# A Fourier layer with a routed mixture of experts: small VectorE steps of gate, ranks and scales fused or given to GpSimd, the inverse's result evicted by either of two engines, constants anew

## The chip, the cores and the metric

The kernel runs on one core of a Trainium2 chip. The metric is device time in microseconds (us), the median of three runs. Five engines work side by side: TensorE (PE in the profile, its weight loads PEld), VectorE (DVE), ScalarE (ACT), GpSimd (POOL) and SyncE (SP), which issues most transfers.

## The reference, cut

```python
def _attn_ref(x, w_r, w_i, b_r, b_i):             # x: 8 x 2496 x 256
    X = np.fft.rfft(x, axis=1)
    Yr = X.real @ w_r - X.imag @ w_i + b_r
    Yi = X.real @ w_i + X.imag @ w_r + b_i
    Y = soft(Yr, 0.01) + 1j * soft(Yi, 0.01)      # sign(v) * max(|v| - 0.01, 0)
    return np.fft.irfft(Y, n=2496, axis=1)

def _moe_ref(x, w_gate, w_output_gate, w1, w2):   # x: 19968 x 256; 8 experts, 1024 wide
    logits = x @ w_gate
    e_idx = np.argmax(logits, axis=1)
    gate_w = softmax(logits)[range(N), e_idx]
    eom = 1 / (1 + exp(-(x @ w_output_gate)))
    for e in range(8):
        m = e_idx == e
        out[m] = gate_w[m] * eom[m, e] * (relu(x[m] @ w1[e]) @ w2[e])
    return out
```

## The kernel before

**Two parts.** Up to about 546 us the kernel runs the Fourier layer and the routing; after it the experts' matmuls. Numbers of full precision are carried as pairs of f16 (a high part and the rest), so most products are three matmuls, and most results are evicted from PSUM by two engines: ScalarE writes the high part, VectorE the rest.

**The Fourier layer** goes batch by batch (8 of them), several batches in flight. A batch's 2496 = 39 x 64 points are transformed in two steps: `stage1_pair` (matmuls L722, evicted into `at` by ScalarE L741 and VectorE L742), a turn (transposes L803 into `A`, evicted by L807 or L808, ScalarE or VectorE), `stage2` (matmuls L839, evicted into `xt` by L850 and L851). Then `mix`: ScalarE seeds a PSUM bank with the bias (L871), PE adds the spectral products onto it (24 matmuls of L895 to a bank), ScalarE and VectorE make the soft threshold (L914, L915), L921 to L923 split it, PE does the inverse's first step (L931, L937, L940; 12 short matmuls to a bank), and that is evicted into `bt` by ScalarE L955 and VectorE L956 and into the short `ste` by L957 or L958. PE cannot start L895 of a bank before its seed, and ScalarE does its instructions in the order of its queue. `stage4` does the inverse's second step (L1006); its result `yt` is evicted by ScalarE alone (L1010, 88 times in all) and stored.

**Gate, ranks, scales.** For each batch `scales` works out powers of two for its values, `gate` the softmax, the chosen expert as a one-hot tile (`goh`, and `oh` as f16) and the factor `gf`; `rank` counts each token's place within its expert: PE sums the one-hot tile over tokens (L1124 to L1129, using the pair sums `two` and `four`), VectorE adds what earlier batches counted (`cnt`) and splits the rank into a part above 128 (`rhi`) and a part below (`rlo`). Nearly all of these are VectorE instructions on tiles of 117 x 22 or 117 x 176. `weights` scales the experts' sixteen weight blocks: two ScalarE squares a block (L1189), the maximum over partitions by a diagonal (L506), one matmul and a reduce, and then a high and a low part of each quarter (L1207 to L1212, ScalarE, GpSimd or VectorE), stored to DRAM.

**The experts.** 160 tiles of 128 tokens are gathered (GpSimd's indirect DMA, L1575), split, turned by DMA, and multiplied by `w1` (L1712) and `w2` (L1671), in two phases: 64 tiles of the first four batches, then the rest, for which `routing` runs again meanwhile.

**What sets the order.** The order of every engine's instructions is worked out when the kernel is built, by a planner (class `Issue`): each step asks for an engine with a due time and an assumed duration, and an engine that is free takes, of what is ready, the step that is due first. The due times are sums of constants (`P`, `SD`, `YE` and so on). A step may offer several engines, each with a constant of its own, and the first that takes it does it.

Of the kernel before, what the change touches and what calls it, by code (L numbers as in the profile page):

```python
# [153 lines left out]
S2 = 36.19
E1 = 82.57
DS = 4.85
ES = 34.56
Z1 = 12.24
SD = 132.3
Z2 = -21.33  # L160
IV = 103.61
IS = 2.48
GO = -1340.85
R0 = 141.78
R1, G1 = -1014.28, 0.61
GA = 0.73
W0 = 43.28
W1 = 19.43
TG = 1016.93
# [15 lines left out]
LR = 1668.96  # L185
QN, QY, QV, QX, QZ, QU = 3866.14, 1364.73, 1212.64, 805.81, -550.14, 1685.64
RA, QE = 1801.63, 933.82
SA = 944.74
SE = 31.03
Z3 = 233.71  # L190
BE = 2815.69
YE = -619.08
PB = 0.39, 14.59, 85.72, 5.95, 22.66, 102.66, 62.64, -123.59
O0 = 1223.31, -1027.38, 1422.52, -7.66, 35.14, -414.49, 54.41, 251.39
O1 = 1875.42, -636.5, -63.9, -292.47, 1069.7, -70.5, 1004.15, 899.13
O2 = 1839.52, -6.84, 1018.92, -1092.03, 4.43, 1897.44, 1747.57, -106.55
O3 = -364.35, -986.35, -931.95, -936.43, -1557.73, -1082.43, -727.4, 454.49
O4 = -1854.58, -1035.4, 1670.63, 1274.07, 1014.79, -952.98, -211.38, -1425.86
# [3 lines left out]
WF = -1.9
QO = 909.37
WHL = 850.77
RG = 1206.15
QG = 1153.73
# [1576 lines left out]
```

## Time and profile before

| | us |
|---|---|
| median of 3 runs | 1391.66 |
| lowest, highest | 1390.07, 1393.12 |
| profiled execution | 1396.24 |
| its span, first to last instruction | 1394.5 |
| mean granted clock of TensorE | 0.997 |
| TensorE busy | 1368.5 (98%) |
| VectorE busy | 981.9 (70%) |
| ScalarE busy | 749.3 (54%) |
| GpSimd busy | 611.8 (44%) |

The profiled execution took 4.58 us more than the median, and 1.74 us more than its span. The busy shares are averages over the two parts of the kernel, which have different limits; the table of stretches tells them apart. In a timeline "idle before" is the time for which the engine stood still ahead of the instruction, with the instruction that ended it behind the arrow.

### The profile page before, as it was taken

How to read it: one execution, taken by the hardware profiler on the slowest of the kernel's cores; microseconds unless marked ns; L12 is line 12 of the kernel's file. 1: busy time of each engine (PE TensorE's matmuls, PEld its weight loads, DVE VectorE, ACT ScalarE, POOL GpSimd, SP SyncE). 2: the span in 40 equal slices, each digit the busy share in tenths (PEclk: the TensorE clock that was granted, in tenths of full speed). 3: DMA queues.
4: the chain of work that ended last, by engine and by line, in shares of the span. 5: the costliest groups of instructions: out<-in, count | busy, mean ns of one | idle time of the engine just before them, and what ended most of it. 6: DMA issues, size and time to landing. Idle time of an engine off the chain costs nothing.

```text
span 1394.5 us, 40372 instructions
## 1 busy us (share of the span) xinstructions
PE 1368.5 (98%) x15528; PEld 1229.4 (88%) x15528; DVE 981.9 (70%) x2852; ACT 749.3 (54%) x1443; POOL 611.8 (44%) x703
## 2 busy tenths in 40 slices
PE   8999999999999999999999999999999999999998
PEld 8998898898888888898998988899999899999997
DVE  6888888889998977788888865554555455554551
ACT  6778787978787764433333343433333343433342
POOL 2374446446676642354444434333333333333322
PEclk9999999999999999999999999999999999999999
DMA  8597999998997889884452464454542655537540
GB/s 248 133 219 215 205 243 213 255 226 207 256 211 179 192 257 170 254 203 138 130 137 74 114 157 117 102 167 108 166 105 73 170 156 140 138 74 200 129 118 30
DMA packets 280546, 231.11 MB, mean 166 GB/s; under 512 B 233076, under 2 KB 242039, under 8 KB 273954
## 3 DMA queue, kind: packets, MB, share of 16 engines
q1 hardware_dynamic: 264735, 186.68, 53.7%
q0 software_dynamic: 15344, 41.77, 11.6%
q8 instruction: 122, 2.00, 0.6%
q14 instruction: 71, 0.57, 0.2%
q10 hardware_dynamic: 274, 0.09, 0.0%
HBM read 285.30 MB, written 58.45 MB: 247 GB/s over the span
## 4 chain that ended last, share of the span: by engine, by line
PE 83%; DVE 5%; issue 5%; ACT 3%; DMA 2%; POOL 1%; SPq 0%; POOLq 0%; DVEq 0%; ACTq 0%
PE ps L1712 28%; PE ps L1671 28%; PE ps L895 12%; PE ps L722 4%; PE ps L1006 3%; PE ps L839 3%; PE ps L940 2%; PE ps L937 1%; POOL out L1691 1%; PE ps L1474 1%; PE ps L1052 1%; DMA x<-in_x 1%; ACT junk L1189 1%; DVE bt L956 1%; DVE xt L851 0%
## 5 line engine op out<-in xcount | busy, mean ns | idle before, releaser
L1671 PE MATMUL ps<-wbuf,hh 128*128 128x256 f16 x3408 | 415.2, 273 | 0.0
L1712 PE MATMUL ps<-eT,wbuf 128*128 128x256 f16 x3408 | 412.9, 273 | 1.2 <-issue 0.7
L1723 DVE SCALAR_TENSOR_TENSOR hh<-ps,hh 128x512 f16<-128x512 f32 x284 | 196.1, 690 | 262.6 <-ACT hh L1722 218.1
L1712 PEld LDWEIGHTS <-wbuf 128*128 128x128 f16 x3408 | 330.3, 98 | 44.2 <-issue 6.0
L1671 PEld LDWEIGHTS <-hh 128*128 128x128 f16 x3408 | 330.7, 98 | 38.8 <-issue 0.4
L1722 ACT ACTIVATE hh<-ps 128x512 f16<-128x512 f32 x284 | 169.6, 597 | 338.4 <-PE ps L1712 294.0
L1691 POOL DMA_INDIRECT out<-o,sidx x160 | 163.0, 1019 | 260.3 <-ACT o L1688 232.4
L1575 POOL DMA_INDIRECT yg<-yd,gidx x160 | 158.5, 991 | 262.0 <-DVE yhl L1602 219.6
L895 PE MATMUL ps<-whl,xt 128*128 128x256 f16 x1824 | 213.6, 274 | 4.4 <-ACT ps L871 4.2
L895 PEld LDWEIGHTS <-xt 128*128 128x128 f16 x1824 | 176.5, 98 | 27.8 <-issue 5.2
L1688 ACT ACTIVATE o<-ps,facs 128x256 f32<-128x256 f32 x160 | 75.9, 474 | 96.3 <-PE ps L1671 83.1
L1601 ACT ACTIVATE yhl<-yg,ys 128x256 f16<-128x256 f32 x160 | 78.6, 502 | 51.5 <-DVE ys L484 14.5
L722 PE MATMUL ps<-f1t,x 117*128 117x120 f32 (+1 forms) x704 | 85.0, 277 | 2.0 <-DVE at L742 1.8
L722 PEld LDWEIGHTS ps<-f1t,x 117*128 117x128 f32 x704 | 82.0, 192 | 4.8 <-DVE at L742 2.8
L1602 DVE SCALAR_TENSOR_TENSOR yhl<-yg,ys,yhl 128x256 f16<-128x256 f32 x160 | 79.7, 507 | 5.5 <-issue 3.7
L1211 POOL TENSOR_TENSOR wsp<-wr,wsp 128x512 f16<-128x512 f32 x57 | 68.2, 1197 | 4.7
L914 ACT ACTIVATE zhl<-ps,sc 128x512 f32<-128x512 f32 (+1 forms) x80 | 54.0, 675 | 27.1 <-PE ps L895 25.6
L839 PE MATMUL ps<-ct,A 128*128 128x128 f16 x944 | 65.0, 222 | 2.4 <-DVE A L789 1.9
L923 POOL TENSOR_TENSOR zhl<-z,zhl 128x512 f16<-128x512 f32 (+1 forms) x51 | 59.3, 1163 | 16.0 <-ACT zhl L921 14.5
L1006 PE MATMUL ps<-bdt,f4t 120*117 120x512 f16 x264 | 65.8, 379 | 0.0
L475 DVE TENSOR_REDUCE yms<-yg 128x1 f32<-128x256 f32 x160 | 61.8, 409 | 5.7 <-DMA yg<-yd,gidx 5.7
L839 PEld LDWEIGHTS <-A 128*128 128x128 f16 x944 | 57.6, 99 | 5.7 <-ACT A L788 2.1
(260 smaller groups left out, 2017.6 us busy)
## 6 DMA issues: line engine op xcount, KB each, us to landing
wbuf<-wd SPq DMA_DIRECT2D x142, 1024.0 KB
latebt<-wd SPq DMA_DIRECT2D x36, 1024.0 KB
latebdt<-wd SPq DMA_DIRECT2D x34, 1024.0 KB
yd<-yt SPq DMA_DIRECT2D x40, 475.3 KB
x<-in_x SPq DMA_DIRECT2D x40, 468.0 KB
wr<-in_moe_w SPq DMA_DIRECT2D x32, 512.0 KB
wd<-wsp SPq DMA_DIRECT2D x64, 256.0 KB
yg<-yd,gidx POOLq DMA_INDIRECT x160
```

Of the source, the lines that this page charges most:

```text
L722: T.matmul(pv[:, dh, :, 6 * j:6 * j + (6 if g + j < 11 else 2)], xs[:P3, j0 + j, 128 * dh:128 * dh + 128], fw, start=True, stop=True)
L839: T.matmul(pt[:, 128 * (2 * dh + j):128 * (2 * dh + j) + 128], a[:, (k1 + j) % KP, dh, v], ct[:, k1 + j, vc], start=(v + vc == 0), stop=(( ...
L895: T.matmul(yp[:, 256 * j:256 * j + 256], xt_[:, v, 2 * dh + j, 64 - 64 * u:192 - 64 * u], whl[:, dh, vw, 256 * u:256 * u + 256], stop=(j = ...
L1006: T.matmul(pt[:P3], w, src[:, :, :, vb_], start=(n == 0), stop=(n == 2))
L1575: yield "G", r + 5.6 * POS[t] - 30, 1.3, lambda: G.indirect_dma_start(out=yg, out_offset=None, in_=src, in_offset=bass.IndirectOffsetOnAxi ...
L1601: yield "A", r - 10, 0.5, lambda: A.activation(yhl[:, 0], yg[:, :256], AF.Copy, scale=s)
L1602: yield "D", r - 10, 0.48, lambda: V.scalar_tensor_tensor(yhl[:, 1], yg[:, :256], s, yhl[:, 0], ALU.mult, ALU.subtract)
L1671: T.matmul(st["pt", t][1][c * q:c * q + c, :256], hh[:, v, fc, 128 * n + c * q:128 * n + c * q + c], wq[:, fc // 2, vw, fc % 2], start=(fc ...
L1691: yield "G", r - DN, 1.3, lambda: G.indirect_dma_start(out=outs[POS[t] % 8], out_offset=bass.IndirectOffsetOnAxis(ap=sidx[:rows, t:t + 1], ...
L1712: T.matmul(pt[:, 128 * m * j + 64 * q:128 * m * j + 64 * q + n], wq[:, dh, g // 4, vw, 128 * (g % 4):128 * (g % 4) + 128], tok, start=(k = ...
L1722: yield "A", r, 0.6, lambda: A.activation(hv[:, 0], pt, AF.Relu)
L1723: yield "D", r, 0.69, lambda: V.scalar_tensor_tensor(hv[:, 1], pt, 0.0, hv[:, 0], ALU.max, ALU.subtract)
```

## The change

**Gate and ranks.** A maximum with 0.5, a comparison and a cast (L1095, L1096, L1098 of before) become one VectorE instruction that writes `oh` directly (L1100 of after). The addition of 1e-9 goes to GpSimd (`floor`, L1115), the pair sums `two` and `four` too (L1125, L1126), the copy into `cnt` and the product of one-hot tile and rank (L1147, L1148), and the rank's high part, now rounded by adding and taking away 1.5 x 2^23 (`ROUND`) in three GpSimd instructions (L1153 to L1155) in place of a shift; the low part is one VectorE instruction (L1156). By the rows of the two programs, a batch has 18 small VectorE instructions of gate, ranks and scales fewer and 4 new ones, and 11 new GpSimd instructions.

**Weights.** The sum of a block's two squares and the diagonal go to GpSimd (L1196, L513), the scale's inverse is worked out once for all blocks in `factors`: 62 VectorE instructions fewer, 32 GpSimd instructions more.

**The inverse's result.** `yt` may be evicted by ScalarE or by VectorE: 50 times L1013 (ScalarE) and 38 times L1014 (VectorE), where before it was L1010 88 times.

**Constants.** All of the planner's constants are new, and with them the order on every engine and some of the choices between engines: 28 squares of x on ScalarE (L630) for 20 (L621), 27 evictions of `A` on VectorE for 23, 14 low parts of weights on VectorE for 7. TensorE runs the same matmuls. In all VectorE has 2695 rows for 2828, ScalarE 1362 for 1393, GpSimd 811 for 709. Line numbers shift: L955 is L957 in the changed kernel, L914 L916, L871 L873, L742 L744, L1189 L1195.

```diff
+ROUND = 12582912.0
-P = 76.09
+P = 95.76
...
@@ scales
             V.tensor_scalar(sc[:, 0:1], st[b, "sx"], sw, 2.0 ** -12, ALU.mult, ALU.mult)
-            V.tensor_scalar(sc[:, 7:8], st[b, "sxi"], swi, 2.0 ** 6, ALU.mult, ALU.mult)
...
-            V.tensor_scalar(sc[:, 5:6], sc[:, 7:8], st["sg"][0], 32.0 / S, ALU.mult, ALU.mult)
-            V.tensor_scalar(sc[:, 6:7], sc[:, 7:8], st["sg"][1], -32.0 / S, ALU.mult, ALU.mult)
...
+        yield "G", r + 5, 0.5, multi(
+            lambda: G.tensor_scalar(sc[:, 7:8], st[b, "sxi"], swi, 2.0 ** 6, ALU.mult, ALU.mult),
+            lambda: G.tensor_scalar(sc[:, 5:6], sc[:, 7:8], st["sg"][0], 32.0 / S, ALU.mult, ALU.mult),
+            lambda: G.tensor_scalar(sc[:, 6:7], sc[:, 7:8], st["sg"][1], -32.0 / S, ALU.mult, ALU.mult))
@@ stage4
-            yield "A", r - YE, 0.6, lambda: A.activation(y[:, q % 4:q % 4 + 2, 0:256], pt[:P3].rearrange("p (a d) -> p a d", a=2), AF.Copy, scale=32.0 / S)
+            yield [("A", r - YE, 0.6, lambda: A.activation(yd_, yp_, AF.Copy, scale=32.0 / S)),
+                   ("D", r - YE + QI, 0.68, lambda: V.tensor_scalar(yd_, yp_, 32.0 / S, None, ALU.mult))]
@@ gate
+        io.go(floor(b, r, ss))
         yield "D", r, 0.33, lambda: V.tensor_reduce(mx, oh, AX.X, ALU.max)
-        yield "D", r, 0.6, lambda: V.tensor_scalar(mx, mx, 0.5, None, ALU.max)
-        yield "D", r, 0.55, lambda: V.tensor_tensor(oh, oh, bc(mx), ALU.is_equal)
-        yield "D", r, 0.62, multi(
-            lambda: V.tensor_copy(ohb, oh),
-            lambda: V.tensor_tensor(L, LO[:, :, E:], oh, ALU.mult))
+        yield "D", r, 0.55, lambda: V.scalar_tensor_tensor(ohb, oh, 0.5, bc(mx), ALU.max, ALU.is_equal)
+        yield "D", r, 0.33, lambda: V.tensor_tensor(L, LO[:, :, E:], ohb, ALU.mult)
...
-        yield "D", r, 0.8, multi(
-            lambda: V.tensor_scalar(ss, ss, 1e-9, None, ALU.add),
-            lambda: V.scalar_tensor_tensor(ss, eo, 1.0, ss, ALU.add, ALU.mult))
+        yield "ss", b
+        yield "D", r, 0.4, lambda: V.scalar_tensor_tensor(ss, eo, 1.0, ss, ALU.add, ALU.mult)
...
+    def floor(b, r, ss):
+        yield "G", r, 0.25, lambda: G.tensor_scalar(ss, ss, 1e-9, 1.0, ALU.add, ALU.mult)
+        io.set("ss", b)
@@ rank
-        yield "D", r, 0.7, multi(
-            lambda: V.tensor_tensor(two, ohb[:, :, 0], ohb[:, :, 1], ALU.add),
-            lambda: V.tensor_tensor(four, tw[:, :, 0], tw[:, :, 1], ALU.add))
+        yield "G", r, 0.7, multi(
+            lambda: G.tensor_tensor(two, ohb[:, :, 0], ohb[:, :, 1], ALU.add),
+            lambda: G.tensor_tensor(four, tw[:, :, 0], tw[:, :, 1], ALU.add))
...
-            lambda: V.tensor_copy(cnt[b], rank[:, NQ]),
-            lambda: V.tensor_tensor(oh, oh, rank[:P3, :NQ], ALU.mult))
+        yield "G", r, 0.75, multi(
+            lambda: G.tensor_copy(cnt[b], rank[:, NQ]),
+            lambda: G.tensor_tensor(oh, oh16[:, b, :NQ], rank[:P3, :NQ], ALU.mult))
...
+        yield "G", r, 0.65, multi(
+            lambda: G.tensor_scalar(ri, rr, 2.0 ** -7, -127 / 256, ALU.mult, ALU.add),
+            lambda: G.tensor_scalar(ri, ri, ROUND, 1.0, ALU.add, ALU.mult),
+            lambda: G.tensor_scalar(rhi[:, qs], ri, -ROUND, 1.0, ALU.add, ALU.mult))
+        yield "D", r, 0.3, lambda: V.scalar_tensor_tensor(rlo[:, qs], rhi[:, qs], -128.0, rr, ALU.mult, ALU.add)
@@ weights
-            yield "D", r, 0.1, lambda: V.tensor_reduce(mm, mx, AX.X, ALU.add)
-            yield from allmax(ma, mm, r)
...
+            yield "G", r, 0.2, lambda: G.tensor_tensor(mm, mx[:, 0:1], mx[:, 1:2], ALU.add)
+            yield from allmax(ma, mm, r, e="G")
+            s = swe[:, u:u + 1]
+            yield "D", r, 0.75, lambda: root2(ma, "swe", to=s)
```

Place A is in ScalarE's queue, at about 113 us of the trace of before, where the second batch is mixed. Before (`ps`, `zhl` and `A` with numbers are single buffers; the last row is the seed of the next bank):

```order
L955 ACTIVATE bt<-ps_1937 128x40x12
L1189 ACTIVATE junk,wmx_1931<-wr_1738 128x1024
L957 ACTIVATE ste<-ps_1937 128x4x8
L955 ACTIVATE bt<-ps_1954 128x40x12
L914 ACTIVATE zhl_1951<-ps_1539,sc_927 128x512
L955 ACTIVATE bt<-ps_1982 128x40x12
L914 ACTIVATE zhl_1972<-ps_1573,sc_927 128x512
L957 ACTIVATE ste<-ps_1954 128x4x8
L850 ACTIVATE xt_1865<-ps_1905 128x4x128
L807 ACTIVATE A_2001<-ps_2004 128x512
L807 ACTIVATE A_2001<-ps_2010 128x512
L871 ACTIVATE ps_2042<-bs_1009 128x512
```

The same place in ScalarE's queue of after:

```order
L957 ACTIVATE bt<-ps_1890 128x40x12
L957 ACTIVATE bt<-ps_1906 128x40x12
L916 ACTIVATE zhl_1920<-ps_1562,sc_872 128x512
L959 ACTIVATE ste<-ps_1890 128x4x8
L959 ACTIVATE ste<-ps_1906 128x4x8
L916 ACTIVATE zhl_1982<-ps_1578,sc_872 128x512
L957 ACTIVATE bt<-ps_1967 128x40x12
L873 ACTIVATE ps_1999<-bs_930 128x512
```

Before, ten rows stand between the first eviction and the seed, a square of the weights among them; after, six. In PE's queue 48 short matmuls (24 of L940, 24 of L803) stand there before, and after 76, of which 24 are of the long L895.

Place B is in VectorE's queue, at about 237 us, where a gate and its ranks meet the evictions of another batch's first transform (`at`). Before:

```order
L1119 TENSOR_TENSOR two<-oh_168 117x96
L1120 TENSOR_TENSOR four<-two 117x48
L742 SCALAR_TENSOR_TENSOR at<-ps_4105,sx_3564,at 128x40x12
L1106 TENSOR_SCALAR gs<-gs 117x22
L1107 SCALAR_TENSOR_TENSOR gs<-ge,gs 117x22
L1135 TENSOR_TENSOR gx<-ps_4152,cnt_2919 128x184
L1108 RECIPROCAL gs<-gs 117x22
L1141 COPY cnt_4177<-gx 128x8
L1142 TENSOR_TENSOR goh<-goh,gx 117x176
L1109 TENSOR_SCALAR gf_4042<-gs,sc_1634 117x22
L1143 TENSOR_REDUCE gr<-goh 117x22
L742 SCALAR_TENSOR_TENSOR at<-ps_4117,sx_3564,at 128x40x12
```

After:

```order
L1108 SCALAR_TENSOR_TENSOR gs<-ge,gs 117x22
L1109 RECIPROCAL gs<-gs 117x22
L853 SCALAR_TENSOR_TENSOR xt_4004<-ps_4011,xt_4004 128x4x128
L1141 TENSOR_TENSOR gx<-ps_4046,cnt_2907 128x184
L1110 TENSOR_SCALAR gf_3962<-gs,sc_1671 117x22
L853 SCALAR_TENSOR_TENSOR xt_4029<-ps_4031,xt_4029 128x4x128
L1149 TENSOR_REDUCE gr<-goh 117x22
L744 SCALAR_TENSOR_TENSOR at<-ps_4057,sx_3517,at 128x40x12
L744 SCALAR_TENSOR_TENSOR at<-ps_4066,sx_3517,at 128x40x12
L1156 SCALAR_TENSOR_TENSOR rlo<-rhi,gr 117x22
```

Before, nine rows of the gate lie between two evictions of `at`; after, the gate stands ahead of these evictions, and only L1156 lies among them.

Place C is in ScalarE's queue, at about 311 us, where the fifth batch is mixed. Before:

```order
L1189 ACTIVATE junk,wmx_5330<-wr_5116 128x1024
L914 ACTIVATE zhl_5372<-ps_5111,sc_3558 128x512
L914 ACTIVATE zhl_5435<-ps_5156,sc_3558 128x512
L955 ACTIVATE bt<-ps_5419 128x40x12
L871 ACTIVATE ps_5473<-bs_3576 128x512
```

After:

```order
L957 ACTIVATE bt<-ps_5372 128x40x12
L957 ACTIVATE bt<-ps_5388 128x40x12
L916 ACTIVATE zhl_5401<-ps_4972,sc_3511 128x512
L959 ACTIVATE ste<-ps_5372 128x4x8
L957 ACTIVATE bt<-ps_5405 128x40x12
L959 ACTIVATE ste<-ps_5388 128x4x8
L916 ACTIVATE zhl_5418<-ps_5045,sc_3511 128x512
L923 ACTIVATE zhl_5401<-z_5402 128x512
L959 ACTIVATE ste<-ps_5405 128x4x8
L873 ACTIVATE ps_5437<-bs_3577 128x512
```

Before, the seed follows one eviction; after, nine rows of evictions and thresholds stand ahead of it, and in PE's queue 24 matmuls of L940 and seven longer ones stand between the first of these evictions and the matmuls that need the seed.

## Rows read from the trace of the kernel before

**Rows 1.** The page's part 1: busy us, share of the span, instructions.

```profile
PE 1368.5 (98%) x15528; PEld 1229.4 (88%) x15528; DVE 981.9 (70%) x2852; ACT 749.3 (54%) x1443; POOL 611.8 (44%) x703
```

**Rows 2.** Stretches: length, busy us (instructions) of five engines, PE clock, DMA share, GB/s.

```profile
0.00:30.00 30.00, 25.97 (x246) 24.14 (x247) 17.96 (x51) 18.30 (x32) 8.42 (x16) 0.94 0.83 247
...
111.00:160.00 49.00, 45.16 (x559) 39.14 (x558) 41.30 (x109) 39.18 (x80) 22.22 (x31) 0.97 0.82 196
...
222.00:267.00 45.00, 42.03 (x449) 37.15 (x447) 34.64 (x80) 35.12 (x69) 22.52 (x29) 1.00 0.97 241
267.00:351.00 84.00, 82.86 (x1046) 75.15 (x1045) 75.85 (x203) 69.48 (x136) 43.87 (x59) 1.00 0.96 218
351.00:499.00 148.00, 145.29 (x1748) 129.61 (x1746) 138.09 (x335) 118.31 (x230) 97.34 (x125) 1.00 0.88 213
499.00:546.00 47.00, 43.42 (x474) 37.36 (x471) 33.90 (x108) 25.81 (x56) 20.71 (x24) 1.00 0.86 223
546.00:1100.00 554.00, 553.77 (x5797) 496.41 (x5795) 380.01 (x1243) 219.58 (x421) 224.72 (x233) 1.00 0.53 139
1100.00:1394.50 294.50, 288.49 (x3595) 260.09 (x3593) 142.47 (x451) 110.77 (x213) 99.31 (x101) 1.00 0.48 125
```

**Rows 3.** Timeline of PE, 111 to 123 us: start, duration, line, [idle before].

```profile
115.16 0.83 PE L940 MATMUL ps<-gt,zhl 128*128 128x128 f16 x12 [1.11 <-ACT ste L957]
...
117.33 1.85 PE L803 MATMUL ps<-t,at 128*128 128x128 f16 x16 [0.63 <-ACT ste L957]
119.28 4.45 PE L895 MATMUL ps<-whl,xt 128*128 128x256 f16 x24
```

**Rows 4.** Timeline of ACT, 106 to 121 us.

```profile
113.42 0.57 ACT L955 ACTIVATE bt<-ps 128x480 f16<-128x480 f32 x1 [0.16 <-PE ps L940]
113.88 1.05 ACT L1189 ACTIVATE junk<-wr 128x1024 fp8e5<-128x1024 f32 x1
...
118.58 0.66 ACT L871 ACTIVATE ps<-bs 128x512 f32<-128x512 f32 x1
```

**Rows 5.** Timeline of PE, 232 to 246 us.

```profile
237.56 0.20 PE L1126 MATMUL ps<-two,t 117*128 117x96 f16 x1 [0.67 <-DVE two L1119]
...
242.07 1.15 PE L722 MATMUL ps<-f1t,x 117*128 117x120 f32 x8 [1.64 <-DVE at L742]
```

**Rows 6.** Timeline of DVE, 230 to 246 us.

```profile
232.13 0.53 DVE L1095 TENSOR_SCALAR gm<-gm 117x22 f32<-117x22 f32 x1
...
236.69 0.82 DVE L1119 TENSOR_TENSOR two<-oh 117x96 f16<-117x96 f16 x1
...
239.46 0.86 DVE L1141 COPY cnt<-gx 128x8 f32<-128x8 f32 x1
...
243.23 0.18 DVE L1149 CAST rhi<-gri 117x22 f16<-117x22 int32 x1
```

**Rows 7.** Timeline of POOL, 230 to 246 us.

```profile
236.29 1.16 POOL L1211 TENSOR_TENSOR wsp<-wr,wsp 128x512 f16<-128x512 f32 x1
```

**Rows 8.** Groups of ACT by line and shape: count | busy, mean ns | idle before.

```profile
L1010 ACT ACTIVATE yt<-ps 117x512 f32<-117x512 f32 x88 | 52.0, 597 | 7.5 <-PE ps L1006 5.3 <-DMA yd<-yt 0.4
...
L914 ACT ACTIVATE zhl<-ps,sc 128x512 f32<-128x512 f32 x72 | 49.4, 686 | 24.7 <-PE ps L895 23.2 <-PE ps L1006 0.7 <-POOL wr L1210 0.4
...
L955 ACT ACTIVATE bt<-ps 128x480 f16<-128x480 f32 x80 | 45.2, 571 | 12.3 <-PE ps L940 5.5 <-PE ps L937 4.7
...
L957 ACT ACTIVATE ste<-ps 128x32 f32<-128x32 f32 x57 | 11.1, 200 | 5.4 <-DVE bt L956 5.0
```

**Rows 9.** Groups of DVE by line and shape.

```profile
L808 DVE CAST A<-ps 128x512 f16<-128x512 f32 x23 | 15.5, 684 | 3.9 <-PE ps L803 3.8
```

**Rows 10.** One line of DVE: ns shortest/median/longest, first and last start.

```profile
L1106 DVE TENSOR_SCALAR gs<-gs x8: 166/168/1131, 111.6 to 545.1; 117x22 f32<-117x22 f32 x8
```

**Rows 11.** Groups of POOL by line and shape.

```profile
L1018 POOL COPY yt<-gf 117x4 f32<-117x4 f32 x40 | 8.1, 218 | 9.5 <-DVE gf L1109 9.5
```

**Rows 12.** Timeline of DVE, 506 to 512 us.

```profile
508.94 0.42 DVE L475 TENSOR_REDUCE yms<-yg 128x1 f32<-128x256 f32 x1 [4.63 <-DMA yg<-yd,gidx]
```

More of the change, by code (lines that the diff above doesn't have):

```diff
@@ L147 @@
 ORDERED = {ET.PE, ET.Activation, ET.DVE, ET.Pool, ET.SP}
-P = 76.09
-TP, TE, QT = 2.92, -236.53, 28.34
+P = 95.76
+TP, TE, QT = -221.44, -683.81, -501.89
 PT = (0, 1, 2, 3, 6, 8), (0, 1, 3, 6)
-DK = 3.74
+DK = 1.8
 T1 = 0.91
[L154 to L169, printed above, removed]
+S2 = 74.26
+E1 = 995.04
+DS = 180.79
+ES = 214.07
+Z1 = 117.8
+SD = 380.09
+Z2 = -10.4
+IV = 293.57
+IS = -214.16
+GO = -2453.82
+R0 = 187.87
+R1, G1 = -379.18, 0.92
+GA = 0.09
+W0 = 351.27
+W1 = -130.83
+TG = -80.95
 HEAD = 14.5
@@ L175 @@
 TAILS = dict(x=8.5, y=4.6, A=4.6, b=3.5, r=6.5, s=4.0, e=3.8)
-XL, TA, TB, YS, WL, WS = 1533.53, -25.75, -297.38, 385.98, -474.08, -3331.35
+XL, TA, TB, YS, WL, WS = 2395.07, 4.57, 927.81, 1283.7, 712.99, -1515.65
 EARLY = dict(yg=3, yhl=2, eT=1, hh=1, o=1)
@@ L184 @@
 S1 = 4
[L185 to L198, printed above, removed]
+LR = 4170.29
+QN, QY, QV, QX, QZ, QU = 5904.22, 2236.72, 1562.35, 1795.5, 809.72, 3943.2
+RA, QE = 1843.23, 2082.21
+SA = 1318.38
+SE = 170.03
+Z3 = 693.9
+BE = 3284.12
+YE = -1002.13
+PB = 407.28, 367.65, 362.59, 51.06, -164.9, -44.01, 59.12, 163.19
+O0 = 1139.47, -1191.87, 5178.53, 162.39, 501.03, 311.98, 232.13, 1159.29
+O1 = 2155.62, -947.78, -352.13, 73.01, 1547.68, -470.4, 1129.53, 1750.81
+O2 = 1226.3, -725.89, 996.78, -797.6, 133.77, 2746.98, 5570.01, -1425.54
+O3 = -1318.4, -1073.81, -3205.21, -1668.65, -3045.93, -307.35, -1518.76, 1880.58
+O4 = -2714.29, -1232.29, 958.11, -100.53, -224.91, 1849.45, -1119.96, -1690.47
 XC = 5.0, 2.6, 1.8, 3.4, 1.8, 1.0
-RT = 2761.24
+RT = 3596.71
 WT = 0.0
[L202 to L206, printed above, removed]
+WF = 339.64
+QO = 2950.71
+WHL = -1666.2
+RG = 562.43
+QG = 1459.31
+QI = -392.01
 CB = 4
@@ L432, in tile_fft_moe @@
     isc = pc.tile([128, E], F32, name="isc")
+    swe = pc.tile([128, 2 * E], F32, name="swe")
     A.activation(isc, cnt[-1], AF.Exp)
@@ L487, in pow2, with root2 @@
         return s, inv
-    def root2(m, name, top=9):
+    def root2(m, name, top=9, to=None):
         c = small(1, "p2c", bufs=2)
@@ L495, in root2, with allmax @@
         V.tensor_scalar(e, e, -1.0, float((380 + top) << 22), ALU.mult, ALU.add)
+        if to is not None:
+            V.tensor_scalar(to.bitcast(I32), e, 0x7F800000, None, ALU.bitwise_and)
+            return
         s = small(1, name)
         V.tensor_scalar(s.bitcast(I32), e, 0x7F800000, None, ALU.bitwise_and)
-        inv = small(1, name + "i")
+        inv = small(1, name + "i", bufs=4)
         V.tensor_scalar(inv.bitcast(I32), s.bitcast(I32), -1.0, float(254 << 23), ALU.mult, ALU.add)
         return s, inv
-    def allmax(dst, src, r, dg="dg"):
+    def allmax(dst, src, r, dg="dg", e="D"):
         yield slots[dg]
         d = small(128, dg, BF16, bufs=1)
-        yield "D", r, 0.3, lambda: V.tensor_scalar(d, eye, src, None, ALU.mult)
+        if e == "G":
+            yield "G", r, 0.4, lambda: G.tensor_scalar(d, eye, src, 1.0, ALU.mult, ALU.mult)
+        else:
+            yield "D", r, 0.3, lambda: V.tensor_scalar(d, eye, src, None, ALU.mult)
         def f(i):
@@ L1139, in rank @@
         cnt[b] = ring(pc, [128, E], F32, "cnt", 2)
-        yield "D", r, 0.4, multi(
-            lambda: V.tensor_copy(cnt[b], rank[:, NQ]),
-            lambda: V.tensor_tensor(oh, oh, rank[:P3, :NQ], ALU.mult))
+        yield "G", r, 0.75, multi(
+            lambda: G.tensor_copy(cnt[b], rank[:, NQ]),
+            lambda: G.tensor_tensor(oh, oh16[:, b, :NQ], rank[:P3, :NQ], ALU.mult))
         yield "D", r, 0.33, lambda: V.tensor_reduce(rr, oh, AX.X, ALU.add)
-        ri = psm.tile([P3, 3, NQ], I32, tag="gri", name="gri", bufs=1)
-        yield "D", r, 0.18, lambda: V.tensor_copy(ri[:, 0], rr)
-        yield "D", r, 0.6, multi(
-            lambda: V.tensor_scalar(ri[:, 1], ri[:, 0], 7, None, ALU.arith_shift_right),
-            lambda: V.tensor_scalar(ri[:, 2], ri[:, 0], 127, None, ALU.bitwise_and),
-            lambda: V.tensor_copy(rhi[:, b * NQ:(b + 1) * NQ], ri[:, 1]),
-            lambda: V.tensor_copy(rlo[:, b * NQ:(b + 1) * NQ], ri[:, 2]))
+        ri = psm.tile([P3, NQ], F32, tag="gri", name="gri", bufs=1)
+        qs = slice(b * NQ, (b + 1) * NQ)
+        yield "G", r, 0.65, multi(
[3 more added lines that the diff above has]
+        yield "D", r, 0.3, lambda: V.scalar_tensor_tensor(rlo[:, qs], rhi[:, qs], -128.0, rr, ALU.mult, ALU.add)
         io.set("ranked", b)
```

19 lines of the change are left out of this document (5 added, 14 removed).

## The prediction

> **What bounds the kernel now.** I read the page's busy shares first, then the table of stretches, then the timelines of the stretches in which TensorE stands still. TensorE is busy for 98% of the span [rows 1]; no other engine passes 70%. From 546 us on, in the experts' part, it is idle for 0.23 us of 554 and 6.01 us of the last 294.5 [rows 2], and the change leaves that part's instructions as they are. So what VectorE or ScalarE saves there costs and gains nothing, and only TensorE's idle time ahead of 546 us can be won, or new idle time be made. By length less PE busy that is 4.03 us in 0 to 30 (the start), 3.84 in 111 to 160, 2.97 in 222 to 267, 1.14 in 267 to 351, 2.71 in 351 to 499 and 3.58 in 499 to 546 [rows 2]. In 111 to 160 the granted clock is 0.97 besides: 49 x 0.03 = 1.5 us more, lost in a stretch at 1.2 GHz right behind two waits, in which 24 matmuls of L895 take 4.45 us [rows 3].
>
> **VectorE and GpSimd: what goes.** 18 small VectorE instructions a batch become 4, so 8 x 14 = 112 go, and 62 go at the weights. Their shortest kind takes 0.168 us when nothing holds it up [rows 10], so at least 174 x 0.168 = 29 us of VectorE go. 38 evictions of `yt` come to it; the nearest row of VectorE for such a tile (512 f32 out of PSUM, scaled or cast) is 0.684 us [rows 9], so 38 x 0.684 = 26 us come. VectorE is as full as before. ScalarE loses 38 x 0.597 = 22.7 us [rows 8] and gets eight squares back, some 1.05 us each [rows 4], so 14 us are left. GpSimd gets 11 x 8 + 32 = 120 instructions; its smallest copy takes 0.218 us [rows 11], so some 26 us, on an engine that is busy 44%. None of these sums is time on TensorE. They count at the places where TensorE waits for one of these engines.
>
> **Term (a), place A, the wait behind the square.** TensorE waits 1.11 and 0.63 us for `ste` evictions [rows 3], because ScalarE does a square of 1.05 us between two of them [rows 4]; then L895 waits for its seed (118.58 + 0.66, [rows 4]) until 119.28. From the eviction at 113.42 to the seed's end are 5.8 us of ScalarE, beside 48 short matmuls. In the new order the square has left; eviction, eviction, threshold, two `ste`, threshold, eviction and seed are 3 x 0.571 + 2 x 0.686 + 2 x 0.200 + 0.66 = 4.1 us [rows 4, 8], and 76 matmuls stand beside them, 24 of them long ones. At the rate of the twelve L940 at 115.16, which leave 0.83 us for 12, the 52 short ones are 3.6 us, and the 24 long ones, even at half their time of 4.45 us, 2.2 more: 5.8 us of cover for 4.1. The waits go, and the half clock behind them should go with them. All that can be won here is 3.84 + 1.5 = 5.3. I take -4.0, since some of the 3.84 lies behind 124 us in small waits; bounds -5.3 and 0.
>
> **Term (b), place B, the gate among the evictions of `at`.** TensorE waits 0.67 us for `two` and 1.64 us for L742 [rows 5], because VectorE does nine gate instructions between two evictions, several of them stretched to 0.5 to 0.9 us [rows 6]. Eleven of the rows from L1095 at 232.13 (0.53) to L1149 at 243.23 (0.18) go, 4.2 us together [rows 6], and the gate now stands ahead of these evictions, which follow each other. L1126 now waits for GpSimd instead. I take -2.3, both waits; bounds -3.0 (all of the stretch's idle time) and +0.5 (`two` late by a GpSimd row that is in the way, 1.16 [rows 7], in place of the 0.67).
>
> **Term (c), place C, a new knot.** Before, the seed stands right behind one eviction. After, three evictions, two thresholds, three `ste`, a cast and the seed are 3 x 0.571 + 2 x 0.686 + 3 x 0.200 + some 0.63 + 0.66 = 5.0 us on ScalarE [rows 4, 8] (the cast, which has no row here, is put a little under a threshold). TensorE has 24 matmuls of L940 beside that, 1.3 to 1.7 us at the rate of 115.16, and seven longer ones, some 0.2 us each by L895 at 119.28 [rows 3], 1.3. So it stands still for some 2.3 us, which I take; bounds 0, if these evictions run ahead of TensorE's order by as much, and +4.5, if the clock falls behind the wait as it did in 111 to 160 [rows 2].
>
> **Term (d), 26 us of evictions in a full queue.** In 351 to 499 VectorE is busy 138.09 of 148 us [rows 2], the fullest stretch, and `yt` evictions fall there too. They take the place of small steps of about the same sum, but a piece of 0.684 us is longer than one of 0.168. I take +0.5; bounds -1 (the stretch's 2.71 us of idle go in part) and +4 (they come to more than double).
>
> **Term (e), what is left ahead of 499 us.** Other seeds and evictions come earlier or later with the new constants, ScalarE with 14 us less work. TensorE's idle time that is left is the start's 4.03 and small waits. I take -0.5, bounds -1 and +1.
>
> **Term (f), 499 to 546.** VectorE, and TensorE after it, waits for the first gather, 4.63 us at 508.94 [rows 12]; the transfers that lead there keep their order. 0, bounds -1 and +1.5. **Term (g), the experts' part.** The second phase's routing matmuls come later in TensorE's order, by 38 us of its work, and the tiles that need their result stand where they stood; in the order of after three pairs of tiles lie between, where seven lay. By TensorE's order alone that holds. 0, bounds 0 and +3.
>
> **The sum.** -4.0 - 2.3 + 2.3 + 0.5 - 0.5 = -4.0 us, so the profiled execution's 1396.24 would be 1392.2. The median of the runs shown is 4.58 us below that execution; the same 4.0 off the median of 1391.66 gives 1387.7.
>
> **Rival 1: the knot only moves.** Each order that a planner deals out has its knots, and mine are three looked at among many. If place C costs 3.6 us (the whole 5.0 less the short matmuls) and (d) 1.5 us, the sum is -4.0 - 2.3 + 3.6 + 1.5 = -1.2: 1390.5, no difference. For it: before, there are two clear knots, and the new order shows one already. Against it: ScalarE, behind which (a) and (c) stand, has 14 us less to do.
>
> **Rival 2: VectorE's queue stands still for GpSimd; slower.** Each batch now has three places where VectorE's next instruction waits for a result of GpSimd: L1108 for the sum with 1e-9, L1149 for the product, L1156 for `rhi`. GpSimd takes its queue in order, and one row of the weights' split ahead of the step is 1.16 us [rows 7]. Behind the waiting instruction stand the evictions of `at`, `xt` and `bt` on which TensorE depends. Three waits of up to 1.16 us in 8 batches are 28 us; the four gates that fall in 267 to 499 have 14 of them, and VectorE has 8.15 + 9.91 = 18 us to spare there [rows 2], much of it not where it is wanted. If TensorE feels half of the 14, the sum is -4.0 + 7 = +3, and the median 1395. It decides from a mean of about 0.6 us a wait. The trace already shows the two engines holding each other up: L1119 takes 0.82 us from 236.69, and so ends at 237.51 when a GpSimd subtraction of 1.16 us from 236.29 ends at 237.45 [rows 6, 7]. The Trainium skill (SBUF — State Buffer, "SBUF: two separate sides") says that the two engines share a pair of ports as an exclusive lock, held for a whole instruction, and this row agrees; the same page lets GpSimd wait for VectorE as well, so by that rule each of the 120 new GpSimd rows can hold a VectorE row, or be held by one, for 0.2 us and more, which speaks against the change. Against this rival: in most cases other VectorE rows stand between a GpSimd step and the one that needs it (L1149 has three between it and L1141 at place B), and the new rows are short.
>
> **Rival 3: all knots loosen.** (a) -5.3, (b) -2.6, (c) 0, (d) -1, (f) -1: -10 in round figures, 1381.7. For it: ScalarE and VectorE lose stretched steps everywhere, and both ends are within the idle time of the trace. Against it: it needs every place to go well at once.
>
> **How the numbers follow.** The forecast has a chance of 0.42, rival 1 0.23, rival 2 0.18, rival 3 0.17. Some 0.2% (2.8 us) is what a measurement of this kernel can tell from no change, so faster means below 1388.9 and slower above 1394.4. The forecast's own spread, from its bounds about 3 us either way, lies on both sides of 1388.9, with some five parts in six below; that is 0.36, and with rival 3 0.17 and a little of rival 1 it makes 0.54 for faster, the rest of both 0.28 for no difference, and rival 2 0.18 for slower. The range reaches from 1380.0, a little under rival 3, to 1395.5, a little over rival 2; below it and above it lie some 0.08 and 0.10.
>
> **What would show it.** Right: in 111 to 160 the clock is 1.00 and TensorE's idle time under 1 us; in 222 to 267 no wait of L722 for `at` over 0.5 us; at about 311 us a wait of L895 for a seed of 2 to 3 us; VectorE's busy time within 10 us of 982, ScalarE's some 14 us under 749. Rival 2: VectorE's L1108, L1149 and L1156 with waits for GpSimd of more than 0.6 us in the mean, and TensorE waiting for L744, L853 or L958 behind them. Term (g) wrong: idle time of TensorE between 800 and 1130 us, ended by a gather. What would make the whole prediction wrong is a knot that I did not look at: a wait of several us of TensorE, at a place where the order of after differs and none of the rows above stands.

## The result, and the profile after

The changed kernel takes 1403.48 us (median of 4 runs) where the kernel before takes 1392.11 in runs of the same chip: a ratio of 1.0088, interval 1.0074 to 1.0102. It is slower by 0.9%, where 0.3% faster was forecast. The page's busy times go the way of the sums, not all by their size: ScalarE is at 737 us for 749 (14 less was forecast), GpSimd at 631 for 612 (26 more was forecast), VectorE at 967 for 982 (about as full as before was forecast), TensorE the same [rows 1].

```profile
PE 1369.0 (98%) x15528; PEld 1229.2 (88%) x15528; DVE 967.1 (69%) x2720; ACT 736.9 (53%) x1420; POOL 630.6 (45%) x805
```

The stretches of [rows 2], now of the changed kernel (length, busy us of PE, PEld, DVE, ACT, POOL, PE clock, DMA share, GB/s):

```profile
111.00:160.00 49.00, 49.00 (x620) 44.17 (x619) 40.91 (x91) 40.12 (x81) 30.03 (x51) 1.00 0.98 235
...
222.00:267.00 45.00, 43.32 (x446) 38.50 (x444) 36.41 (x80) 35.84 (x67) 21.42 (x41) 1.00 1.01 244
267.00:351.00 84.00, 77.81 (x967) 69.83 (x965) 67.86 (x166) 62.88 (x123) 47.89 (x74) 0.98 0.91 208
351.00:499.00 148.00, 142.34 (x1682) 126.49 (x1681) 132.42 (x283) 113.46 (x220) 94.42 (x141) 0.99 0.89 206
499.00:546.00 47.00, 43.05 (x478) 37.13 (x476) 34.39 (x107) 26.42 (x55) 21.32 (x26) 0.96 0.86 228
546.00:1100.00 554.00, 551.73 (x5777) 494.56 (x5776) 374.19 (x1230) 217.80 (x417) 227.73 (x240) 1.00 0.54 139
```

In 111 to 160 TensorE is idle for 0.00 us (3.84 before) at full clock; place A is gone. In 222 to 267, with place B, it is 1.68 for 2.97. From 267 us on it is worse in every stretch: 6.19 us idle for 1.14, 5.66 for 2.71, 3.95 for 3.58, 2.27 for 0.23, and the granted clock falls in three of them. What TensorE waited for (us in total, times, longest):

```profile
PE ps L939 <- DVE zhl L917: 5.2, 2, 5.0
PE ps L897 <- ACT ps L873: 2.2, 3, 1.7
PE ps L841 <- DMA A<-at: 2.1, 1, 2.1
PE ps L1474 <- DVE ob L1466: 2.1, 2, 1.9
...
PE ps L1712 <- DMA wbuf<-wd: 1.7, 1, 1.7
```

One wait of 5.0 us stands out. It is place C. The timeline of TensorE there:

```profile
303.45 1.88 PE L942 MATMUL ps<-gt,zhl 128*128 128x128 f16 x30
310.36 2.07 PE L939 MATMUL ps<-gt,zhl 128*128 128x128 f32 x8 [5.03 <-DVE zhl L917]
```

That of ScalarE, in the order that the change's section shows:

```profile
304.18 1.09 ACT L957 ACTIVATE bt<-ps 128x480 f16<-128x480 f32 x2 [0.18 <-PE ps L942]
305.16 0.68 ACT L916 ACTIVATE zhl<-ps,sc 128x512 f32<-128x512 f32 x1
...
306.83 0.68 ACT L916 ACTIVATE zhl<-ps,sc 128x512 f32<-128x512 f32 x1
```

And that of VectorE:

```profile
307.22 0.64 DVE L958 SCALAR_TENSOR_TENSOR bt<-ps,bt 128x480 f16<-128x480 f32 x1
307.79 0.34 DVE L1227 TENSOR_TENSOR pfA<-pfA,fl 128x1 f32<-128x1 f32 x2
308.16 1.14 DVE L1250 TENSOR_SCALAR pfA<-pfA 128x9 f32<-128x9 f32 x1
...
309.62 0.68 DVE L917 SCALAR_TENSOR_TENSOR zhl<-ps,zhl 128x512 f32<-128x512 f32 x1
```

GpSimd at the same time:

```profile
308.11 1.16 POOL L925 TENSOR_TENSOR zhl<-z,zhl 128x512 f16<-128x512 f32 x1 [0.45 <-ACT zhl L923]
```

TensorE has done its short matmuls by 305.33 and needs the second threshold. ScalarE's half (L916) of it comes at 306.83, behind evictions, and VectorE's half (L917) at 309.62, behind more evictions and five rows of the routing's plan. One of these five, L1250, takes 1.14 us beside the GpSimd row, where the same row takes 0.17 in e13; about 1 us of the wait is this row.

To add the places up, I take the start of each matmul less the matmul work that stands ahead of it in TensorE's queue (each kind at the spacing it has where nothing waits). What this delay grows by in a stretch is what TensorE loses there, waits and slow clock together. The stretches go by work done, so that two orders can be compared; 280 us of work is at 300 us of time in the changed kernel, 500 at 548. The sizes hang on the spacing that is taken, so only differences between columns are read; and the wait at 474 us stands at the border of 440, so the rows on either side of it are best read together. Losses in us:

| work done | before | e9 | changed | e16 | e13 |
|---|---|---|---|---|---|
| 0 to 100 | 11.1 | 10.1 | 12.8 | 15.2 | 14.9 |
| 100 to 280 | 17.0 | 15.1 | 6.7 | 6.7 | 6.7 |
| 280 to 300 (place C) | 0.4 | 0.4 | 7.3 | 8.7 | 2.6 |
| 300 to 440 | 8.3 | 8.2 | 14.6 | 16.6 | 15.2 |
| 440 to 560 | 6.4 | 4.3 | 9.4 | 7.6 | 7.9 |
| 560 to the end | 5.2 | 3.1 | 3.1 | 3.1 | 3.1 |

(e9, e13 and e16 are runs below: before with three rows moved, the changed kernel with place C mended, the changed kernel again.) Up to 280 us of work the change wins 8.6 us; behind it, it loses 16.2 up to 560.

### The profile page after: what moved, and what is told of

The parts are those of the page before. It is cut to its first block, busy times and chain, and to the rows that moved or that the text cites. A ratio compares the mean times of both kernels' runs of the same rounds, so it can differ in the third digit from the quotient of the medians.

```text
span 1400.0 us, 40323 instructions
## 1 busy us (share of the span) xinstructions
PE 1369.0 (98%) x15528; PEld 1229.2 (88%) x15528; DVE 967.1 (69%) x2720; ACT 736.9 (53%) x1420; POOL 630.6 (45%) x805
## 4 chain that ended last, share of the span: by engine, by line
PE 54%; issue 4%; POOL 1%; DMA 0%; POOLq 0%; ACT 0%; ACTq 0%
PE ps L1712 27%; PE ps L1671 26%; POOL out L1691 1%; PE ps L1474 1%; DMA eT<-yhl 0%; PE ps L1008 0%; POOL yg L1575 0%; POOLq L1779 0%; POOLq L1693 0%; ACT hh L1722 0%; POOLq L1691 0%; DMA wbuf<-wd 0%; POOLq L1575 0%; ACTq L1722 0%
## 5 line engine op out<-in xcount | busy, mean ns | idle before, releaser
L897 PE MATMUL ps<-whl,xt 128*128 128x256 f16 x1824 | 211.9, 273 | 2.2 <-ACT ps L873 2.2
L897 PEld LDWEIGHTS <-xt 128*128 128x128 f16 x1824 | 176.3, 98 | 26.0 <-issue 3.9
L1602 DVE SCALAR_TENSOR_TENSOR yhl<-yg,ys,yhl 128x256 f16<-128x256 f32 x160 | 75.6, 482 | 5.8 <-ACT yhl L1601 5.5
L916 ACT ACTIVATE zhl<-ps,sc 128x512 f32<-128x512 f32 (+1 forms) x80 | 54.0, 675 | 31.9 <-PE ps L897 27.7
L853 DVE SCALAR_TENSOR_TENSOR xt<-ps,xt 128x512 f16<-128x512 f32 x80 | 54.1, 682 | 11.3 <-ACT xt L852 10.7
```

The source lines that it names most:

```text
L897: T.matmul(yp[:, 256 * j:256 * j + 256], xt_[:, v, 2 * dh + j, 64 - 64 * u:192 - 64 * u], whl[:, dh, vw, 256 * u:256 * u + 256], stop=(j = ...
L1602: yield "D", r - 10, 0.48, lambda: V.scalar_tensor_tensor(yhl[:, 1], yg[:, :256], s, yhl[:, 0], ALU.mult, ALU.subtract)
```

## The experiments

Ratios are to the kernel before in runs of the same chip, with their intervals.

**Code or order?** e1 is the old code with the new constants, e2 the new code with the old ones (`yt` on ScalarE alone).

> The kernel before with the planner's new constants and nothing else of the change (all small steps on VectorE, all 88 evictions on ScalarE). Theory (the loss is in places where the new constants put work in a bad order): slower than before, 1396 to 1410 us, with new waits of TensorE of over 1.5 us behind 267 us. Rival (the loss is in the code: steps on GpSimd, evictions on VectorE): 1380 to 1390 us, since the order of the first 300 us is the one that gained some 8 us there.

> The changed code of gate, ranks, scales and weights with the constants of before; the 88 evictions all on ScalarE. Theory: about as before, 1386 to 1396 us, VectorE some 45 us less busy than in before. Rival (GpSimd's steps hold up VectorE's queue): 1397 us and more, with VectorE waiting for GpSimd at the sum, product and high rank for over 0.6 us in the mean.

```diff
e1:  all constants as in the changed kernel, nothing else
e2:  all constants as before
-            yield [("A", r - YE, 0.6, ...), ("D", r - YE + QI, 0.68, ...)]
+            yield "A", r - YE, 0.6, ...
```

e1 is 1.0378 (1.0358 to 1.0398), e2 1.0328 (1.0309 to 1.0348). Both are far worse than either kernel, e2 against what I expected of it, and e1 (1445 us) well beyond the 1410 that I put as the most. e15 shows that dealing the work anew is enough for a loss of this kind:

> The kernel before with a single one of the planner's constants changed, by half a microsecond (the distance of two batches, P, from 76.09 to 76.59), so that the work is dealt out anew. Theory (an order fits only the code and the constants that it was chosen with, and any other is worse by a per cent and more): 1405 us and more. Rival (the 3 per cent of the two runs with crossed code and constants come from their mismatch, not from dealing anew): within 0.5% of before.

```diff
-P = 76.09
+P = 76.59
```

1.0205 (1.0192 to 1.0218): half a microsecond on one constant of the kernel before costs 2%. So three times an order that was dealt out with constants not chosen for its code is worse by 2 to 3.8%, once with no change of the code at all. The changed kernel, with its own constants, is at 1.0088, where its code (but for the choice of engine for `yt`) with the old constants is at 1.0328.

**The parts in a fixed order.** Here the planner goes through the same steps with the same assumed times, and only what a step emits, or on which engine, is changed.

> The new small steps (fused on VectorE, or on GpSimd) in the order of before: TensorE's, ScalarE's and SyncE's queues are those of before row for row, VectorE's lacks 174 rows, GpSimd's has 120 more, and all 88 evictions stay on ScalarE. Theory (the steps gain, the new order loses): 1384 to 1390 us, the waits of 0.67 and 1.64 us at 237 to 242 us half gone or more, the knot at 113 us as before. Rival (passing steps to GpSimd holds up VectorE): 1393 us and more.

> As the run before this one, and every second eviction of the inverse's result (40 of 88) emitted on VectorE at the same place of the program. Theory (evictions on VectorE gain a little, as putting them back on ScalarE lost 2 us in the changed kernel): 1 to 3 us under the run before. Rival (in an order not dealt for them they stand in VectorE's way): 1 to 6 us over it.

> The changed kernel with its order kept, only the 38 evictions that VectorE does are emitted on ScalarE at the same places of the program. Theory (the evictions are not the loss): no gain, 1402 to 1412 us, since ScalarE gets 22.7 us more and stands at most of the knots. Rival (26 us of evictions in VectorE's queue make the loss): 1393 to 1399 us, with the wait of 5.03 us at 305 us gone or halved.

> The changed kernel with its order kept, only the 120 instructions moved to GpSimd (gate, ranks, scales, weights) are emitted on VectorE at the same places of the program. Theory (the passing to and from GpSimd costs next to nothing): 1401 to 1408 us; the wait of 1.9 us at 361 us, behind the last step of a rank, shrinks by 1 us or more, other waits change by small amounts. Rival (VectorE's queue stands still for GpSimd): 1390 to 1398 us.

```diff
e5 (on the kernel before, cut; steps and assumed times kept, what they emit as in the changed kernel):
-        yield "D", r, 0.6, lambda: V.tensor_scalar(mx, mx, 0.5, None, ALU.max)
+        yield "D", r, 0.6, lambda: None
...
-            lambda: V.tensor_tensor(two, ohb[:, :, 0], ohb[:, :, 1], ALU.add),
+            lambda: G.tensor_tensor(two, ohb[:, :, 0], ohb[:, :, 1], ALU.add),
e6 (on e5), for every second pair:
+                yield "A", r - YE, 0.6, lambda: V.tensor_scalar(yd_, yp_, 32.0 / S, None, ALU.mult)
e3 (on the changed kernel):
-                   ("D", r - YE + QI, 0.68, lambda: V.tensor_scalar(yd_, yp_, 32.0 / S, None, ALU.mult))]
+                   ("D", r - YE + QI, 0.68, lambda: A.activation(yd_, yp_, AF.Copy, scale=32.0 / S))]
e4 (on the changed kernel, cut), the 120 GpSimd instructions:
-            lambda: G.tensor_tensor(two, ohb[:, :, 0], ohb[:, :, 1], ALU.add),
+            lambda: V.tensor_tensor(two, ohb[:, :, 0], ohb[:, :, 1], ALU.add),
```

e5 is 0.9999 (0.9990 to 1.0008): in the order of before, 174 VectorE instructions fewer and 120 passed to GpSimd come to nothing together; neither the gain of the theory nor the loss of the rival shows, and the run does not take the two apart. TensorE at place B in e5, where L1131 is L1126 of before and L730 is L722:

```profile
238.96 0.20 PE L1131 MATMUL ps<-two,t 117*128 117x96 f16 x1 [0.92 <-POOL two L1124]
...
242.94 1.15 PE L730 MATMUL ps<-f1t,x 117*128 117x120 f32 x8 [0.98 <-DVE at L750]
```

The wait for `two` went from 0.67 to 0.92, that for `at` from 1.64 to 0.98 [rows 5]. e6 is 1.0062 (1.0041 to 1.0083): 40 evictions moved to VectorE without an order dealt for them cost 0.6%, against the small gain that I expected. In the changed kernel's order, undoing its moves does not help: e3 is 1.0103 (1.0086 to 1.0120) and e4 1.0126 (1.0109 to 1.0142), against 1.0088. e4 is slower by more than the intervals leave open, so there the small steps on GpSimd pay; for e3 the intervals overlap. So neither part, taken out of this order, gives the loss back, and VectorE hardly stands still for GpSimd: in the changed kernel these are all of its waits for the new steps, in eight batches:

```profile
DVE rlo L1156 <- POOL rhi L1155: 0.7, 1, 0.7
DVE gr L1149 <- POOL goh L1148: 0.4, 1, 0.4
```

**Single waits of the new order.** A few rows are emitted later than the planner dealt them, all else in place. In the diffs, `HOLD` names an engine, the number of a step in its queue, and how many steps later it is emitted.

> The changed kernel with five rows of VectorE's queue (one piece of the routing's plan) moved behind the soft threshold for which TensorE waits 5.03 us at 305 us. Theory (the plan's rows are 1.8 us of that wait): that wait falls to some 3.3 us and the total by 1.5 to 3.5. Rival (ScalarE's half of the threshold, started at 306.83, is the bound): within 1 us of the changed kernel.

> The changed kernel with place C mended by order alone: on ScalarE two soft thresholds ahead of the three evictions (and their short ones) that they stood among, on VectorE the same two thresholds ahead of three evictions and of five rows of the routing's plan. Theory (the wait of 5.03 us at 305 us is a cause by itself): the wait falls to 1 to 2 us, the half clock behind it goes, and the total falls by 3 to 6 us against the changed kernel of the same chip. Rival (ScalarE and VectorE are behind as a whole, so that the time comes back at the next seeds and evictions): the wait falls, and by 365 us the gain is under 1.5 us, the total within 2 us of the changed kernel.

> The changed kernel itself, as the neighbour of the three runs before on the same chip: 0.7 to 1.0% over before.

```diff
e8 (prefix and plan: the same number of pieces, that with L1250 joined to the next):
             if e % 3 == 2:
                 yield
+                if name == "pfA" and e == 5:
+                    yield
...
-        yield
+        if ph:
+            yield
         for ev, num, start in todo:
e13:
+HOLD = {("A", 398): 2, ("A", 399): 2, ("A", 401): 1, ("A", 402): 1, ("A", 403): 1,
+        ("D", 437): 2, ("D", 438): 2, ("D", 440): 1, ("D", 441): 1}
```

e8 is 1.0073 (1.0057 to 1.0089), too near 1.0088 to tell. Its trace shows the five rows moved, and the wait as long as before, 5.06 us, because in that execution ScalarE stood still for 2.75 us ahead of the first eviction:

```profile
308.61 1.03 ACT L957 ACTIVATE bt<-ps 128x480 f16<-128x480 f32 x2 [2.75 <-issue]
```

The trace has the cause: ahead of this row ScalarE's queue waits for the semaphore of a DMA transpose that still reads `bt` (L982), and that transfer lands at 308.54. In the other traces the first eviction starts as closely behind the same landing: 304.10 and 304.18 us in the changed kernel, 307.22 and 307.29 in e16. From this eviction to TensorE's L939, e8 takes 3.64 us, the changed kernel 6.18 and e16 5.46. So moving the five rows does shorten the chain, by the 1.8 us of the theory against e16, and a buffer that came free late hid it in the traced execution.

e13 moves the evictions on both engines too, and settles it: 1.0039 (1.0026 to 1.0052) beside 1.0091 (1.0076 to 1.0107) for the changed kernel on the same chip, medians 1397.78 and 1404.63. 6.9 us come back by the order of 13 rows. TensorE at place C in e13 (L954 is L939):

```profile
308.86 1.16 PE L954 MATMUL ps<-gt,zhl 128*128 128x128 f32 x8 [1.50 <-DVE zhl L932]
```

ScalarE there (L931 is L916, L972 is L957), the thresholds now ahead of the eviction that waits for `bt`:

```profile
306.06 1.36 ACT L931 ACTIVATE zhl<-ps,sc 128x512 f32<-128x512 f32 x2
307.95 1.03 ACT L972 ACTIVATE bt<-ps 128x480 f16<-128x480 f32 x2 [0.54 <-DMA bdt<-bt]
```

The stretch 267 to 351 us in e13:

```profile
267.00:351.00 84.00, 80.98 (x1022) 72.81 (x1021) 71.30 (x178) 65.73 (x130) 52.48 (x82) 1.00 0.95 217
```

The same stretch in e16:

```profile
267.00:351.00 84.00, 77.78 (x945) 68.97 (x944) 64.86 (x158) 60.56 (x119) 47.23 (x72) 0.94 0.88 201
```

The wait falls from 5.03 to 1.50, the clock is 1.00, and by the table the gain of 6.1 us at place C (8.7 to 2.6) is still there at the end. That is half of the loss: e13 is still 6.5 us over the kernel before (1391.31 in these runs). The other waits did not give way so:

> The changed kernel with two neighbouring transfers of SyncE's queue exchanged, at 469 to 475 us: the transpose of the last batch's first columns into A ahead of a transpose of bt that it stood behind. Theory (this queue order makes the wait of 2.13 us at 474 us, and the half clock behind it): 2 to 4 us under the changed kernel, so 1399.5 to 1401.5. Rival (the time is given back behind it, at the gather): within 1 us of the changed kernel.

> As the run before this one, with two more moves: the transpose into A at 473 us ahead of its neighbour, and four routing matmuls at 361 us behind eight matmuls of the first transform. Theory: each adds its wait, 1 us at 361 and 1.5 to 3 at 474, so 6 to 10 us under the changed kernel. Rival: within 3 us of the changed kernel.

```diff
e7:
+HOLD = {("S", 249): 1}
e14: as e13, and
+        ("S", 249): 1, ("P", 369): 1
```

e7 is 1.0094 (1.0077 to 1.0111), e14 1.0045 (1.0025 to 1.0065): no gain on what they are built on, as far as the intervals tell (about 2 us). The traces of e7 and e8 say less than that: by the table's method they lose 3.8 and 5.6 us between 865 and 885 us, in the experts' part, where the edits move nothing and the changed kernel's trace loses nothing. TensorE in the changed kernel, at the wait that e7 and e14 take away:

```profile
476.83 1.08 PE L841 MATMUL ps<-ct,A 128*128 128x128 f16 x12 [2.13 <-DMA A<-at]
```

TensorE in e14 behind the same matmuls (L906 is L891, L912 is L897):

```profile
475.50 0.86 PE L906 MATMUL ps<-whl,xt 128*64 128x128 f16 x24 [1.01 <-ACT ps L890]
...
482.56 2.78 PE L912 MATMUL ps<-whl,xt 128*128 128x256 f16 x24 [0.51 <-ACT ps L888]
...
515.29 2.78 PE L912 MATMUL ps<-whl,xt 128*128 128x256 f16 x24 [2.88 <-ACT ps L888]
```

The wait for the transpose goes, and waits for seeds stand behind it; the last of these is 1.70 in the changed kernel and 1.02 in e13. The wait at 361 us falls from 1.89 to 1.00. This execution of e14 took 1401.83 us, 5 us over its median, so it does not show what its usual run does.

**The clock behind long waits.**

> The changed kernel with 80 matmuls of 128 columns on constants, results unused, in TensorE's queue ahead of the matmul that waits 5.03 us at 305 us (4.4 us of work in a wait that is there anyway). Theory (a part of the loss is TensorE's clock, which falls to 1.2 GHz behind that wait): the granted clock of the run rises by 0.001 to 0.003, and the total falls by 1.5 to 4 us against the changed kernel, ratio 1.006 to 1.008. Rival (only the idle time itself counts): ratio 1.0088 or a little over, the mean clock unchanged.

> The changed kernel with such matmuls in four waits: 80 at 305 us, 34 at 474, 20 at 529 and 28 at 557. Theory (the clock behind long waits): the mean granted clock rises from 0.991 to 0.996 to 0.997 or more, and the total falls by 4 to 8 us, ratio 1.003 to 1.006. Rival (idle time alone): ratio 1.0088 or over.

> The changed kernel with the two transposes at 469 us exchanged and the matmuls on constants in the other three waits (305, 529, 557 us). Theory (waits and the clock behind them, place by place): 1 to 2 us under the run with four fillers, ratio 1.002 to 1.005. Rival: as the run with four fillers or over it, the exchange being given back.

```diff
e10:
             bp = bank(i)
+            if (b, p) == (4, 4):
+                turning(bp, 80)
e11: as e10, and turning(pt, 34), (pt, 20), (pt, 28) ahead of the matmuls that wait at 474, 529 and 557 us
e12: e11 without the 34, with the exchange of e7
```

e10, e11 and e12 are 1.0113 (1.0093 to 1.0133), 1.0095 (1.0080 to 1.0111) and 1.0094 (1.0081 to 1.0108): the theory falls. In e11 the four runs have a mean granted clock of 0.996 to 0.998 (0.991 to 0.996 in the changed kernel's first four), and the clock behind the filled waits is 1.00; but in its trace it falls to 0.86 in 90 to 100 us and to 0.83 in 340 to 350 instead, and the total is the same. A higher mean clock alone returned no time here. The matmuls on constants at 305 us did not delay the next one themselves: in e11's trace that starts at 312.25, and the threshold that it needs ends at 312.19. Where the rest of e11's time went is open.

**Place A alone, in the kernel before.**

> The kernel before with one move: the square of the weights that stood in ScalarE's queue at place A (113.88 us) goes behind the seed at 118.6, ten rows on, and the two VectorE rows that need its result go three and two rows on. Theory (the knot at place A is that square): the waits of 1.11 and 0.63 us go and the seed comes 1 us earlier, so 1.5 to 4 us under before, ratio 0.997 to 0.999, which would beat both kernels. Rival (the knot is the whole chain of evictions and thresholds, the square only fills it): within 0.1% of before.

```diff
+HOLD = {("A", 137): 10, ("D", 171): 4, ("D", 174): 2}
```

0.9997 (0.9988 to 1.0006). TensorE at place A in e9 (L955 is L940, L818 is L803, L910 is L895):

```profile
113.96 0.83 PE L955 MATMUL ps<-gt,zhl 128*128 128x128 f16 x12 [0.91 <-ACT ste L972]
...
116.13 0.38 PE L818 MATMUL ps<-t,at 128*128 128x128 f16 x4 [0.42 <-ACT ste L972]
...
118.09 2.78 PE L910 MATMUL ps<-whl,xt 128*128 128x256 f16 x24
```

With the square gone the waits are 0.91 and 0.42 for 1.11 and 0.63 [rows 3], and the total is the same: the square was not the cause. That the chain of evictions is, as the rival has it, fits the waits, which still end with its `ste` rows; no run here took it apart. The 24 matmuls of L895 take 2.78 us for 4.45, since the clock did not fall in this execution; of the kernel before's 12 runs beside e13, 11 have a mean clock of 0.999 or 1.000, where its profiled execution has 0.997.

## Why the prediction was wrong, step by step

- **(a) and (b)** were right in place and sign, in the order as it was dealt, and (b) in size. By the table's method place A (100 to 140 us of work) loses 1.4 us for 8.2, -6.8 where -4.0 was forecast and -5.3 was the bound; the 1.9 us by which e9 loses less in its row of the table (15.1 for 17.0) are mostly the fall of the clock in before's execution (4.45 us for 2.78 on the 24 matmuls of L895 above), without which some -5 is left. Place B (200 to 260) loses 3.8 for 6.4, -2.6 for -2.3. The reasons were partly wrong: the square did not make place A (e9), and the removed steps alone took 0.4 us off the two waits at place B (e5); the new order around them did the rest.
- **(c)** is the step that failed most. The place was right, the wait was not: +6.9 us by the table where +2.3 was taken and +4.5 was the bound. I counted "seven longer ones" as work beside ScalarE's chain. Four of these (L939, eight rows in the trace) need the second threshold, which is in that chain, and VectorE's half of it stood behind rows that I had not laid beside it. The cover from the first eviction on (304.18) was 1.15 us of short matmuls, to 305.33, where I had 1.3 to 1.7 and 1.3 of longer ones. e13 shows the price of the order there: 6.9 us of the median.
- **(d) and (e)**, 0 together with bounds -2 and +5: 300 to 440 us of work loses 14.6 for 8.3, +6.3. (d)'s evictions on VectorE are not seen to cause it, since e3 without them is no faster. The trace shows places that I had not looked at: 1.89 us at 361 and 2.13 at 474, with the slow clock behind it (0.86 in 470 to 480 us). At the first of these L1474 waits for VectorE rows that follow both waits for GpSimd above, but rival 2's mechanism does not explain it: in e4, with these steps on VectorE, TensorE still waits 1.67 us for the same kind of row. What makes these losses is not shown: e7 and e14 took waits away, e10 to e12 filled some, and none gave time back beyond what e13 does.
- **(f) and (g)**, 0: 440 to 560 loses 9.4 for 6.4, +3.0, of which 1.7 is a load of expert weights (`wbuf`) at 557 us, a queue that I did not follow; no run tested it. The routing of the second phase costs nothing, as forecast.
- **The start**, not in the sum: 1.7 us more up to 100 us of work, by a wait of 1.5 us for `wg` at 95 us; and the last row of the table, 2.1 less, since a pause of TensorE at 1110 us in before's execution did not come again.
- **One execution for the median.** The profiled executions lie 5.6 us apart, of which the table gives 5.5, the medians 11.4. Before's profiled execution is 4.1 us over the median 1392.11, with falls of the clock at 20 to 30 us (0.83) and at 120 to 130 (0.86), a mean of 0.997; each is 1.7 us of clock, 0.0012 of the span, so the means of 0.999 and 1.000 of most other runs leave room for one such fall at most. The changed kernel's is 1.6 under its own median. I priced place A with a fall of the clock that was one execution's.
- **The rivals.** Rival 2 had the direction right by the wrong mechanism: VectorE waits 1.1 us for GpSimd in all, 0.05 a place where it needed 0.6. The Trainium skill's exclusive lock of VectorE and GpSimd (SBUF — State Buffer, "SBUF: two separate sides") fits rows of after too: L1250 above runs from 308.16 to 309.30, on a GpSimd subtraction from 308.11 to 309.27. In the same section the Trainium skill has VectorE take the shared ports with two inputs from SBUF or in a two-port mode. L1250 reads one tile, and the trace does not show its mode. Whatever the 120 new GpSimd rows cost in this way, e5's total with all of them is that of before. Rival 1, the knot that only moves, was the right mechanism at several times its price at place C; for the other half of the loss the mechanism stays open.
